# The wait for the last store of a one-core decode kernel, moved from SyncE's instruction stream to GpSimd's

## The chip, the cores and the metric

The kernel runs on one core of one Trainium2 chip. A core has five engines, each with an instruction stream of its own: TensorE (PE), VectorE (DVE), ScalarE (ACT), GpSimd (POOL) and SyncE (SP). They are ordered against each other and against the DMA engines by semaphores alone. The metric is the device time of one execution in microseconds. Beside it stands the span, which is the time from the first to the last instruction of the program in a profile; the device time is longer than the span by what lies before the first and behind the last instruction.

## The reference

The reference is one token of a decode step, a block of cached attention and a small gated mixer behind it. Cut to what matters here:

```python
h  = x + _A_ref(_layernorm(x), k_cache, v_cache, wq, wo)      # 32 query heads, 8 cached heads, 16384 positions of 128
h2 = h + _B_ref(_layernorm(h), w1, w2, w3, w4)                # layernorm, gelu, two products of 512 x 1792
return h2                                                     # shape (1, 1, 512), bfloat16
```

The inputs hold 79 MB that must be read from memory, nearly all of it the two caches. The result is 512 numbers, 1 KB.

## The kernel before

The program is collected as a list of operations for each engine and then emitted (`Program.op` and `Program.emit`). An operation names the tiles it reads (`r`) and writes (`w`); from these the class works out which semaphores it has to wait for. On SyncE, ScalarE and GpSimd the operations stand in the order in which they were collected: `_run` emits, for each operation, the waits that are not yet known to be met, and then the operation. So an operation of an engine comes behind every earlier operation of that engine, and an engine that waits does nothing else.

The work itself is four passes over pairs of cached heads (`PAIRS` is 4). For each pair SyncE loads a 4 MB stretch of keys and one of values; VectorE transposes the keys, TensorE makes the scores, VectorE and ScalarE the softmax, TensorE the product with the values, and GpSimd and ScalarE fold the partial results of each pair but the last. Behind the four pairs come the output projection and the two products of the mixer, with their weights loaded into the space that the keys have left.

All large loads go through SyncE's queue. A SyncE load waits until its target tile is free and is then issued; SyncE carries no arithmetic. GpSimd has little to do: constants and masks at the start, two additions and one product for each of the first three pairs, four instructions that do nothing but wait for the values' landing and raise a semaphore for TensorE (line 499, a `nop`), one such for `od` (line 730), and a power of the variance for each layernorm (line 563). The second of these powers is its last instruction.

The end of the program is this. TensorE's last products (line 844) leave the result in one PSUM bank. ScalarE copies one half of it to the tile `fin` (line 849), VectorE the other (line 851), at the same time. SyncE waits for both and issues the store of `fin` to `out` (line 852). The last operation is a `nop` that reads `out` (line 854): it has no work, and it holds the engine on which it stands until the store's semaphore has its full count. The operation is given the semaphore wait itself, so that it appears as one instruction of the sequencer in the profile.

The functions that the change touches follow.

Of the kernel before, what the change touches and what calls it, by code (L numbers as in the profile page):

```python
# [390 lines left out]
def bass_sequential_preLN__gqa_block_cached__mixer_s_mlp__decode_kernel(  # L391
# [13 lines left out]
    with ExitStack() as ctx:  # L405
        sb = lambda name, shape, dt: ctx.enter_context(nc.sbuf_tensor(name, shape, dt))
        ps = lambda name, shape, dt: ctx.enter_context(nc.psum_tensor(name, shape, dt))
        P = Program(nc, ctx)
# [106 lines left out]
        def piece(cuts, m):  # L515
            return [lo <= m < hi for lo, hi in cuts].index(True)
# [52 lines left out]
        for n, (lo, hi) in enumerate(((0, 2048), (2048, NCH * HQ * DH))):  # L569
# [13 lines left out]
            r=["ident", "x4"], w=["quarter"])  # L583
# [9 lines left out]
             r=["ident_f"], w=["swapped"])  # L593

        dve(lambda e: e.tensor_reduce(row32[:, :], ident_f[:, :].rearrange("p (c r) -> p r c", c=4), AX.X, ALU.add),
            r=["ident_f"], w=["row32"])
        dve(lambda e: e.tensor_reduce(maskdd[:, :], ident_f[:, :].rearrange("p (n d) -> p d n", d=4), AX.X, ALU.add),
            r=["ident_f"], w=["maskdd"])
# [6 lines left out]
        for z, m, key, mk in ((zo, rowgh, "zo", "rowgh"), (zd, maskgh, "zd", "maskgh")):  # L605
# [5 lines left out]
            r=["hT", (("st", 0), 0), (("st", 0), 6)] + [("v", 0), ("v", 1)], w=["xn"])  # L611
# [3 lines left out]
        for i, key in enumerate(keys):  # L615
            P.part("query", i)
            for k in range(NCH):
                pe(lambda e, k=k: e.matmul(row[:, bass.ds(P.b, 512)], copies(xn[:, k:k + 1], 128),  # L618
                                           wq_k[:, k, bass.ds(P.c, REP * DH)], start=(k == 0), stop=(k == NCH - 1)),
                   r=["xn"], also=[("v", 0), ("v", 1)], w=["n" if key == "mn" else key], bank=[key])  # L620
        P.part()
        for g in range(2):
            half = banks[64 * g:64 * g + 64, PAIRS * g:PAIRS * g + PAIRS, :].rearrange("p j c -> p (j c)")
            for b in range(2):
# [3 lines left out]
                    r=["n" if x == "mn" else x for x in keys[PAIRS * g:PAIRS * g + PAIRS]], w=["qcol"],  # L628
# [147 lines left out]
        for n, (lo, hi) in enumerate(W4):  # L776
# [4 lines left out]
            r=[("o_m", j) for j in range(PAIRS)], w=["o_f"])  # L781
# [3 lines left out]
        for r_ in range(32):  # L785
# [3 lines left out]
               r=["o_b", ("r", 0, piece(WO, r_))], w=[("O", 0)], bank=[("O", 0)])  # L789
        h_ps, hkey = banks[:, 6, :], "spare0"  # L790
        dve(lambda e: e.tensor_copy(osum[:, :], O_ps[0][:, :]), r=[("O", 0)], w=["osum"] + [("osum", c) for c in range(4)], bank=[("O", 0)])
        for q in range(4):
            pe(lambda e, q=q: e.matmul(h_ps[32 * q:32 * q + 32, 0:128], copies(row32[:, 0:1], 32),
                                       osum[:, q * 128:(q + 1) * 128], start=True, stop=True),
               r=["osum", "row32"], w=[hkey], bank=[hkey])
# [6 lines left out]
            r=["hT", (S, 0)], w=["hc"])  # L802


        for k in range(NCH):
            for q in range(4):
                pe(lambda e, k=k, q=q: e.matmul(s_ps[32 * q:32 * q + 32, 0, 0:FQ], hc[:, k, :],  # L807
                                                w3_sb[:, k, q * FQ:(q + 1) * FQ], start=(k == 0), stop=(k == NCH - 1)),
                   r=["hc", ("r", 1, piece(W3, k))], w=[("s", 0)], bank=[("s", 0)])
# [3 lines left out]
            r=["hr", "xs", (S, 6)], w=["xsum"])  # L813
        unread_f(384)
        for n in range(2):
# [11 lines left out]
           r=["swapped", "xsum"], w=["n"], bank=["mn"])  # L827
        for m in range(NEAR):
# [3 lines left out]
               r=[("hcol", 2 * m // NHC), ("r", 1, len(W3) + piece(W4, m))], w=[("O", 1)], bank=[("O", 1)])  # L832
        dve(lambda e: e.tensor_copy(osum[:, :], O_ps[1][:, :]), r=[("O", 1)], w=["osum"], bank=[("O", 1)])  # L833
        act(lambda e: e.activation(hg[:, 0:256], hcol[:, 0:8, :].rearrange("p m u -> p (m u)"), ACTF.Identity),
            r=[("hcol", 1)], w=["late", ("hg", 0), ("hg", 1)])
# [6 lines left out]
        for m in range(NEAR, NHC):  # L842
            for o in range(4):
# [4 lines left out]
                   r=["late", ("r", 1, len(W3) + piece(W4, m))], w=["n"], bank=["mn"])  # L848
        act(lambda e: e.activation(fin[:, 0:128], n_ps[0:64, 0:128], ACTF.Identity),
            r=["n"], w=[("fin", 0)], bank=["mn"])  # L850
        dve(lambda e: e.tensor_copy(fin[:, 128:256], n_ps[64:128, 0:128]), r=["n"], w=[("fin", 1)])  # L851
        P.op("SP", lambda e: e.dma_start(out[0, 0:1, :].rearrange("o (q j) -> (o q) j", q=2), fin[31:33, :]),
             r=[("fin", 1), ("fin", 0)], w=["out"], dma="out")
        P.op("SP", lambda e: e.nop(), r=["out"])
        P.emit()

    return nc
# [28 lines left out]
```

## Time and profile before

| What | Value |
|---|---|
| device time, median of 3 runs | 189.55 us |
| the three runs | 189.49, 189.55, 190.38 us |
| device time of the profiled execution | 189.68 us |
| span of the profiled execution | 188.4 us |
| mean granted TensorE clock | 0.900 |
| read from memory | 79.17 MB, 420 GB/s over the span |

The profile is of one execution. Its views give times in microseconds from the start of the span. A "q" behind an engine's name means its sequencer: an instruction that waits, branches or issues a DMA, during which the engine itself stays idle. SyncE has only such instructions. A wait is recorded when it ends: the instruction's start is the time at which its semaphores were met, and its duration is what it took from there. A landing is the time at which a DMA's semaphore had its full count.

### The profile page before, as it was taken

The page shows a single profiled execution, that of the slowest core. Times are in us where ns is not written, and L with a number is a line of the kernel's source. Part 1 is how long each engine was busy: PE and PEld are TensorE (multiplying, and loading weights), DVE is VectorE, ACT ScalarE, POOL GpSimd, SP SyncE. Part 2 cuts the span into 40 slices and gives each one's busy share as a digit, 9 for nine tenths or more (in the row PEclk, how much of TensorE's full clock was granted, in tenths as well). Part 3 has the DMA queues.
Part 4 walks back from the last instruction along what each step waited for, and adds up shares of the span by engine and source line. Part 5 has one row for each costly group of instructions (what it writes and reads, how often), then busy time and mean ns, then how long its engine had stood idle before and what let it go on. Part 6 is the DMA issues. An engine that isn't in the chain of part 4 may idle for free.

```text
span 188.4 us, 2420 instructions
## 1 busy us (share of the span) xinstructions
PE 127.7 (68%) x776; PEld 52.7 (28%) x780; DVE 111.5 (59%) x138; ACT 14.2 (8%) x32; POOL 10.6 (6%) x20
## 2 busy tenths in 40 slices
PE   1019700699965604999775019997986999797974
PEld 1003300243322201344332003432432433353332
DVE  4900751999645009998460069994659895443254
ACT  3000000000020200000112000000220000320012
POOL 1900000000000110000002000000003000000010
PEclk9999995599997975699999756999997899999999
DMA  6999999999999999988999999997999999979994
GB/s 239 457 418 445 445 445 445 445 445 445 445 445 445 445 445 445 417 348 348 445 445 445 445 445 445 445 445 334 445 445 445 557 431 445 431 314 396 419 410 163
DMA packets 2461, 79.19 MB, mean 420 GB/s; under 512 B 282, under 2 KB 284, under 8 KB 924
## 3 DMA queue, kind: packets, MB, share of 16 engines
q1 hardware_dynamic: 2452, 79.17, 97.8%
q8 instruction: 1, 0.02, 0.0%
q10 hardware_dynamic: 8, 0.00, 0.0%
HBM read 79.17 MB, written 0.00 MB: 420 GB/s over the span
## 4 chain that ended last, share of the span: by engine, by line
DMA 66%; DVE 31%; PE 1%; issue 1%; SPq 0%; ACT 0%; DVEq 0%
DMA kb<-in_A_k_cache_dram 53%; DVE kt L641 30%; DMA kb<-in_B_w_dram 13%; PE banks L807 1%; SPq L483 0%; DVE osum L833 0%; PE banks L830 0%; PE banks L844 0%; DVE hcol L821 0%; ACT hg L817 0%; PE banks L838 0%; DVE fin L851 0%; DVEq L159 0%; SPq L159 0%
## 5 line engine op out<-in xcount | busy, mean ns | idle before, releaser
L641 DVE STREAM_TRANSPOSE kt<-kb 128x1024 int32<-128x1024 int32 (+1 forms) x49 | 71.8, 1534 | 31.8 <-DMA kb<-in_A_k_cache_dram 31.8
L660 PE MATMUL banks<-kt,qn 128*128 x256 | 67.8, 414 | 0.0
L660 PEld LDWEIGHTS banks<-kt,qn 128*128 x256 | 26.2, 102 | 40.1 <-issue 21.6
L522 PE MATMUL banks<-xn 128*128 128x512 bf16 x90 | 22.0, 381 | 0.6 <-issue 0.6
L654 PE MATMUL banks<-qn 128*128 128x512 bf16 x8 | 3.7, 465 | 27.0 <-DVE kt L641 26.8
L697 PE MATMUL banks<-vb,pt 128*32 128x512 bf16 x256 | 16.1, 408 | 0.0
L618 PE MATMUL banks<-vb,xn 128*128 x32 | 9.1, 454 | 9.4 <-DVE xn L609 9.4
L682 ACT ACTIVATE p_sb<-banks,bias 128x1024 bf16<-128x1024 f32 x4 | 4.5, 1114 | 126.2 <-DVE nmh L678 126.2
L686 DVE STREAM_TRANSPOSE pt<-p_sb 64x1024 bf16<-64x1024 bf16 x8 | 9.9, 1239 | 5.4 <-ACT p_sb L682 5.3
L522 PEld LDWEIGHTS banks<-xn 128*128 128x128 bf16 x94 | 8.8, 99 | 12.2 <-issue 4.1
L670 DVE TENSOR_REDUCE mx<-banks 128x1 f32<-128x1024 f32 x4 | 4.9, 1225 | 8.9 <-PE banks L660 8.9
L697 PEld LDWEIGHTS banks<-vb,pt 128*32 128x32 bf16 x256 | 7.8, 103 | 6.4 <-issue 1.8
L716 POOL TENSOR_TENSOR osum<-osum 128x256 f32<-128x256 f32 x3 | 2.2, 724 | 126.4 <-ACT osum L713 126.4
L625 DVE STREAM_TRANSPOSE kt<-banks 64x1024 f32<-64x1024 f32 x4 | 4.8, 1228 | 7.2 <-PE banks L618 7.2
L654 PEld LDWEIGHTS banks<-qn 128*128 128x128 bf16 x8 | 0.8, 99 | 29.0 <-issue 28.6
L618 PEld LDWEIGHTS banks<-vb,xn 128*128 128x128 bf16 x32 | 3.6, 112 | 14.5 <-issue 12.1
L732 PE MATMUL banks<-od,zo 128*32 128x128 f32 x8 | 1.6, 285 | 7.3 <-POOL od L718 6.1
L674 PE MATMUL banks<-mxd,mean 128*128 128x128 f32 x8 | 2.0, 326 | 5.3 <-DVE mxd L671 5.3
L713 ACT ACTIVATE osum<-banks,rowc 128x128 f32<-128x128 f32 x12 | 3.4, 368 | 20.6 <-PE banks L697 20.6
L705 PE MATMUL banks<-acc,zd 128*32 128x1 f32 x8 | 0.9, 186 | 4.1 <-DVE pt L686 4.0
L606 DVE COPY zo<-rowgh 128x32 f32<-128x32 f32 x1 | 3.6, 3633 | 0.0
L563 POOL TENSOR_TENSOR st<-st,expo 128x1 f32<-128x1 f32 (+1 forms) x2 | 1.3, 634 | 41.2 <-DVE st L561 41.2
(87 smaller groups left out, 50.9 us busy)
## 6 DMA issues: line engine op xcount, KB each, us to landing
kb<-in_A_k_cache_dram SPq DMA_DIRECT2D x2, 4096.0 KB, 20.5
vb<-in_A_wq_dram SPq DMA_DIRECT2D x1, 3584.0 KB, 11.5
kb<-in_A_wo_dram SPq DMA_DIRECT2D x1, 3584.0 KB, 28.5
kb<-in_B_w_dram SPq DMA_DIRECT2D x1, 1792.0 KB, 24.2
kb<-in_B_w_dram SPq DMA_DIRECT2D x1, 896.0 KB, 26.0
kb<-in_B_w_dram SPq DMA_DIRECT2D x1, 640.0 KB, 27.1
vb<-in_A_wq_dram SPq DMA_DIRECT2D x1, 512.0 KB, 3.4
kb<-in_A_wo_dram SPq DMA_DIRECT2D x1, 512.0 KB, 29.4
```

The lines of the kernel that those rows point to most:

```text
L522: P.unread = lambda e: e.matmul(banks[:, 7, :], copies(xn[:, 0:1], 128), copies(xn[:, 0:1], 512), start=True, stop=True)
L606: dve(lambda e, z=z, m=m: e.tensor_copy(z[:, :].rearrange("p (n d) -> p n d", d=4), m[:, :, :].rearrange("p g h -> p (g h)").unsqueeze(2). ...
L618: pe(lambda e, k=k: e.matmul(row[:, bass.ds(P.b, 512)], copies(xn[:, k:k + 1], 128), wq_k[:, k, bass.ds(P.c, REP * DH)], start=(k == 0), s ...
L625: dve(lambda e, g=g, b=b, half=half: e.transpose(qcol[64 * g:64 * g + 64, 2 * b:2 * b + 2, :, :].rearrange("p e m u -> p (e m u)"), half.r ...
L641: P.op("DVE", lambda e, t=t, n=n, at=at: e.transpose(kt[:, t * KP:(t + n) * KP].bitcast(I32), kb_all[:, at:at + n * KP].bitcast(I32)), r=[ ...
L654: pe(lambda e: e.matmul(row[:, bass.ds(P.y, 512)], copies(none, 128), copies(none, 512), start=True, stop=False, skip_group_check=True), r ...
L660: pe(lambda e, n=n: e.matmul(row[:, bass.ds(P.y, 512)], qn[:, n, bass.ds(P.q, 128)], key_piece(P.k, n), start=False, stop=(n == 3), skip_g ...
L670: dve(lambda e: e.tensor_reduce(mx[:, :], s_all, AX.X, ALU.max), r=[("s", 0), ("s", 1)], w=["mx"], **both)
L682: act(lambda e: e.activation(p_sb[:, :], s_all, ACTF.Exp, bias=bias[:, 0:1], scale=float(SCALE), accum_out=acc[:, :]), r=[("s", 0), ("s", ...
L686: dve(lambda e, g=g: e.transpose(pt[64 * g:64 * g + 64, :, :, g, :], p_sb[64 * g:64 * g + 64, :]), r=["p"], w=["pt"])
L697: pe(lambda e, l=l, ct=ct, ch=ch: e.matmul(O_ps[0][32 * ct:32 * ct + 32, :], pt[:, l, ch, :, :].rearrange("p g u -> p (g u)"), tiles[:, l ...
L713: act(lambda e, c=c: e.activation(osum[:, c * 128:(c + 1) * 128], O[:, c * 128:(c + 1) * 128], ACTF.Identity, scale=rowc[:, c:c + 1]), r=[ ...
```

## The change

The last operation, the `nop` that reads `out`, is collected for GpSimd instead of SyncE. Nothing else differs: the store is still issued by SyncE, through SyncE's queue, and its semaphore is the same.

```diff
         P.op("SP", lambda e: e.dma_start(out[0, 0:1, :].rearrange("o (q j) -> (o q) j", q=2), fin[31:33, :]),
              r=[("fin", 1), ("fin", 0)], w=["out"], dma="out")
-        P.op("SP", lambda e: e.nop(), r=["out"])
+        P.op("POOL", lambda e: e.nop(), r=["out"])
         P.emit()
```

SyncE's stream then ends with the store's issue at line 852. GpSimd's stream ends with the wait, behind the power at line 563.

## Prediction

> **What bounds the kernel now.** I read the page's head and its chain of work first, to see whether the end of the program belongs to what sets the time at all, then the timeline of the last microseconds, then the waits of SyncE, then the single lines that the change touches.
>
> ```profile
> span 188.4 us, 2420 instructions
> DMA 66%; DVE 31%; PE 1%; issue 1%; SPq 0%; ACT 0%; DVEq 0%
> DMA kb<-in_A_k_cache_dram 53%; DVE kt L641 30%; DMA kb<-in_B_w_dram 13%; PE banks L807 1%; SPq L483 0%; DVE osum L833 0%; PE banks L830 0%; PE banks L844 0%; DVE hcol L821 0%; ACT hg L817 0%; PE banks L838 0%; DVE fin L851 0%; DVEq L159 0%;
> q1 hardware_dynamic: 2452, 79.17, 97.8%
> ```
>
> The reader is to see that the kernel is bound by its loads: the queue that SyncE feeds keeps the 16 DMA engines at 97.8% of the span, and the chain is loads and key transposes almost throughout. The change touches no load. It stands entirely behind the last product, so its worth has to be read from the last stretch alone.
>
> ```profile
> 182.21 0.97 PE banks L807 x15
> 183.20 0.50 ACT hg L817
> 184.40 0.63 PE banks L830 x7
> 185.80 0.42 PE banks L838 x8
> 186.22 0.28 PE banks L844 x20
> 186.52 0.33 PE banks L844 x8
> 186.87 0.29 DVE fin L851
> ```
>
> These are pieces of the chain in order of time: start, duration, what. Behind the last load the chain is a strict relay, and it ends with the copy to `fin` at 186.87 + 0.29 = 187.16 us. Only the store comes after that:
>
> ```profile
> 187.21 0.33 SPq L852 DMA_DIRECT2D out_dram<-fin  x1
> SPq L854 <- DMA out_dram<-fin: 0.8, 1, 0.8
> L854 SPq EVENT_SEMAPHORE  x1: 17/17/17, 188.4 to 188.4; - x1
> ```
>
> The first row is of the timeline (start, duration), the second of SyncE's waits (total, times, longest), the third of the view of one source line (shortest, median, longest in ns, then first and last start). SyncE issues the store from 187.21 to 187.54 us. It then sits 0.8 us until the store has landed, at about 188.34, and its last instruction takes 17 ns and ends the span at 188.4. Between the issue and the landing no engine works:
>
> ```profile
> 187.55:188.35 0.80, 0.00 (x0) 0.00 (x0) 0.00 (x0) 0.00 (x0) 0.00 (x0) 0.92 0.01 1
> ```
>
> This is the view by windows: five engines, zero instructions each, then the clock, the DMA share and GB/s. So the last 0.8 us are the store's own flight. Whoever waits for it, it can't land sooner, because it is issued by the same engine from the same place behind the same two copies.
>
> The profiled execution took 189.68 us of device time with a span of 188.4, so 1.3 us lie outside of the span: before the first instruction and behind the last. The profile says nothing on how these 1.3 us are divided or which engine makes them. That is where this change can act, and it is the only place.
>
> **The change part by part.** It removes one sequencer instruction from SyncE, 17 ns at the very end (the row of line 854). Nothing stands behind it on SyncE, so nothing is released earlier inside the program. The wait of 0.8 us doesn't vanish; it is done by GpSimd.
>
> It adds one such instruction to GpSimd. Where GpSimd stands at that time:
>
> ```profile
> 181.97 0.71 POOL L563 TENSOR_TENSOR st<-st,expo 128x2 f32<-128x2 f32 x1 [38.10 <-DVE st L561]
> ```
>
> This is its last instruction and ends at 182.68 us. GpSimd is thus free 182.68 to 188.34, that is 5.7 us, before the store has landed. It can't come late to the wait, and it holds nobody up by standing in it, since no operation of GpSimd follows and no other engine waits for one.
>
> Its cost inside the span is the time from the landing to the end of the waiting instruction, on GpSimd instead of SyncE. GpSimd does the same thing four times already, for the values:
>
> ```profile
> L499 POOLq EVENT_SEMAPHORE  x4: 17/17/17, 51.6 to 168.0; - x4
> L483 SPq DMA_DIRECT2D vb<-in_A_v_cache_dram x1: 328/328/328, 140.1 to 140.1; - x1
> DMA to landing us min/median/max: 27.9/27.9/27.9
> L730 POOLq EVENT_SEMAPHORE  x1: 43/43/43, 173.6 to 173.6; - x1
> ```
>
> The instruction takes 17 ns on GpSimd as on SyncE. The last load of values is issued at 140.1 and lands 27.9 us later, at 168.0, and the fourth wait of line 499 is met at 168.0: with rounding of both rows the reaction is under 0.15 us, and it includes a semaphore update that the new wait doesn't have. The dearest wait of that kind on GpSimd (line 730, on two semaphores, with an update) took 43 ns. So in place of 17 ns the span ends with 17 to 43 ns, and up to 0.15 us if the reaction is as slow as the rounding allows. I take 0.02 us, nearest to line 499, which waits for a DMA's semaphore just like the new one. The other end, below nothing, is excluded but for some nanoseconds, since the landing itself is not moved and SyncE's reaction is only from 188.34 to 188.4.
>
> What lies outside of the span is not shown, so I bound it from both sides. **On the side of a gain:** SyncE now ends its stream at 187.54 instead of 188.37. If SyncE has something of its own to do after its last instruction, it can do that in the 0.8 us of the flight. What it can save is at most 0.8 us from such an overlap, or, if SyncE's closing is longer than that and GpSimd's is nothing, still no more than the 0.83 us by which SyncE ends earlier. It also can't be more than the part of the 1.3 us that lies at the end. So the gain is between nothing and 0.83 us, which puts the lower end of the time at 189.68 - 0.83 = 188.85. **On the side of a loss:** whatever GpSimd does after its last instruction is now hidden by the 5.7 us that it has left, and is exposed after the change. The cover for it is gone completely, since GpSimd becomes the last engine. The nearest rows for the price are those of the program's start, where every engine passes through the same kind of bookkeeping:
>
> ```profile
> L871 POOLq INC_SWDGE_SEM  x1: 27/27/27, 0.1 to 0.1; - x1
> L871 POOLq DRAIN  x1: 187/187/187, 0.3 to 0.3; - x1
> L871 POOLq EVENT_SEMAPHORE  x2: 17/17/17, 0.5 to 0.6; - x2
> L871 SPq DRAIN  x1: 7/7/7, 0.0 to 0.0; - x1
> L871 SPq EVENT_SEMAPHORE  x1: 17/17/17, 0.7 to 0.7; - x1
> L589 POOL MEMSET qb<- 128x2496 bf16 x1 | 2.2, 2178 | 0.0
> ```
>
> SyncE's share of the start is a drain of 7 ns and one wait of 17 ns. GpSimd has a drain of 187 ns, an increment of 27 ns and two waits of 17 ns, 248 ns together. If a closing on GpSimd is as much dearer than one on SyncE as the opening, it costs 248 - 24 = 0.22 us more. Part of that drain is the four memsets that it lets finish, and at the end GpSimd has been idle for 5.7 us, so nothing is in flight: the lower bound is no difference. The far bound is a piece of software work on GpSimd as long as its longest instruction, the 2.2 us of line 589. I take 0.05 us, nearer to nothing than to the 0.22 us, because the waits are equal on both engines and the drain has nothing to drain.
>
> The sum against the profiled execution is 188.37 + 0.02 + 1.31 + 0.05, or 189.75 us. That execution is 0.13 us above the median of the runs, so the forecast for a median is 189.6. The changes of 0.07 us are far below what a measurement of this kernel can tell from no change, about 0.5% or 0.95 us.
>
> The start rows bear out that GpSimd takes part in a barrier of all engines: SyncE's wait of line 871 is met at 0.7, just after GpSimd's at 0.6. The Trainium skill, page "Runtime: NRT & Kernel Launch", section "The ~15µs preamble/postamble breakdown", says that behind the kernel the runtime runs another barrier, which waits for all engines, and that its relay costs 44 ns for each of 8 steps. By that rule an engine that comes last but stands early in the relay would pay up to 8 x 44 = 0.35 us more than one that stands at its end, and the sum would be 190.1 as an estimate; it would also leave SyncE little to gain, as its own clean-up comes only after all engines have met. No row of this trace lies behind the last instruction, so the trace can't confirm it.
>
> **The rivals.** *GpSimd closes slowly.* After its last instruction GpSimd has a closing piece that SyncE lacks, and it now starts at 188.4 instead of 182.7. It decides from the point at which that piece is over 0.95 us longer than SyncE's. For it speaks that it would have been invisible so far, being covered by 5.7 us, and that GpSimd's bookkeeping at the start is ten times SyncE's (248 against 24 ns). Against it speaks that those 248 ns are still far from 0.95 us, and that in the five waits it has in this trace GpSimd reacts as fast as SyncE. Its price is between 0.95 us and the 2.2 us of the longest row, 1.5 in the middle: 189.55 + 1.5 = 191.1 us.
>
> *SyncE closes slowly.* SyncE feeds the one queue that carries 79.17 MB, so it may have more to put in order than the others, and it now starts 0.83 us earlier. The full overlap gives 189.55 - 0.83 = 188.7 us, which is 0.44% and just under the bound; together with the scatter of the runs (189.49 to 190.38) it can come out as faster. For it speaks that 1.3 us outside of the span have to be spent by someone, and SyncE is the one that ends last now. Against it speaks that the closing may need all engines, and then nothing can be done early.
>
> *The change doesn't do what it says.* The end of the program may be held by the store itself, or by something that no engine's last instruction decides, so that the place of the wait is of no account: 189.55, which can't be told from the forecast and is counted with it.
>
> **How the numbers follow.** The forecast, no difference that can be told, gets 0.55 (0.05 of it for the change that does nothing). A slow closing of GpSimd gets 0.30: it rests on a price that no row shows, yet its cover of 5.7 us is the one large quantity that the change removes. An early closing of SyncE gets 0.15 as a faster result, since its bound of 0.83 us leaves it little room beyond 0.5%. The predicted time is 189.6 us. The likeliest case alone has 189.2 to 190.1: SyncE's overlap by half on one side, the 0.22 us of the opening with the 0.15 us of the slow reaction on the other. The range that takes in the other cases goes from 188.6, the full overlap with 0.1 us of scatter, to 191.6, some two thirds of the way from 0.95 to 2.2 us of a slow closing (189.55 + 2.05). Left out are the dearest closings, some 0.10 of the slow case's 0.30, and gains beyond the overlap, 0.03.
>
> **What would show it.** In the profile of the changed kernel line 854 must stand on GpSimd's sequencer with a start of about 188.4 and 17 ns, and SyncE's last row must be line 852, ending at 187.5. The landing must again come about 0.8 us after the issue's end, and the span must stay within 0.05 us of 188.4 once the loads' own scatter is taken off. The test of the rivals is the difference between device time and span: 1.3 us if the forecast holds, 2.3 and more if GpSimd closes slowly, 0.5 if SyncE closes early. The prediction would be wrong if that difference moves by over 0.95 us, or if the span itself is longer because the wait on GpSimd is met late, well behind a landing that comes on time.

## The result, and the profile after

The changed kernel takes 190.19 us in the median of 14 runs, the kernel before 189.66 us in 14 runs. The ratio is 1.0026, with a 95% interval from 1.0015 to 1.0038. So the change makes the kernel slower by about 0.5 us: clear of chance over so many runs, and little over half of the 0.95 us that the prediction had taken as what can be told from no change.

The profiled execution of the changed kernel took 190.17 us, and its span is *shorter* than that of before. The page's first line:

```profile
span 188.2 us, 2420 instructions
```

The timeline of the changed kernel's end (start, duration, what) and the view of the line with the wait (shortest, median, longest in ns, then first and last start):

```profile
186.69 0.27 ACT L849 ACTIVATE fin<-banks 64x128 bf16<-64x128 f32 x1 [1.66 <-PE banks L844]
186.69 0.29 DVE L851 CAST fin<-banks 64x128 bf16<-64x128 f32 x1 [1.12 <-PE banks L844]
187.03 0.33 SPq L852 DMA_DIRECT2D out_dram<-fin  x1
```

```profile
L854 POOLq EVENT_SEMAPHORE  x1: 17/17/17, 188.2 to 188.2; - x1
```

The reader is to see that everything inside the program went as before. The store is issued 0.05 us after the copies end. The issue ends at 187.03 + 0.33 = 187.36, and the wait is met at 188.2, some 0.8 us later, as on SyncE; it takes 17 ns, as on SyncE. What has changed lies behind it. Device time less span was 189.68 - 188.4 = 1.3 us and is now 190.17 - 188.2 = 2.0 us.

This difference is the quantity that the rest goes by. It is known for each execution, with the span rounded to 0.1 us, and it scatters much less than the device time, since the scatter of the loads (spans from 188.0 to 189.2 us in the 14 runs of the changed kernel) drops out of it. It also holds what lies before the first instruction, which no view shows apart. No run below changes anything there, so a difference between two runs is read as one at the end. Over these 14 runs it is 1.90 us in the mean, between 1.81 and 2.00. Below, "the rest" is short for device time less span, with its mean and 95% interval.

### The profile page after: what moved, and what is told of

The parts are those of the page before. It is cut to its first block, busy times and chain, and to the rows that moved or that the text cites. A ratio compares the mean times of both kernels' runs of the same rounds, so it can differ in the third digit from the quotient of the medians.

```text
span 188.2 us, 2420 instructions
## 1 busy us (share of the span) xinstructions
PE 128.0 (68%) x776; PEld 52.6 (28%) x780; DVE 111.5 (59%) x138; ACT 14.2 (8%) x32; POOL 10.6 (6%) x20
## 4 chain that ended last, share of the span: by engine, by line
DMA 52%; DVE 27%; PE 18%; issue 1%; SPq 0%; ACT 0%; DVEq 0%; POOLq 0%
DMA kb<-in_A_k_cache_dram 52%; DVE kt L641 24%; PE banks L660 8%; PE banks L522 4%; PE banks L697 2%; PE banks L787 1%; DVE mx L670 1%; DVE od L727 1%; PE banks L807 1%; PE banks L530 1%; SPq L483 0%; DVE osum L791 0%; DVE osum L833 0%; PE banks L830 0%; PE banks L844 0%
## 5 line engine op out<-in xcount | busy, mean ns | idle before, releaser
L660 PE MATMUL banks<-kt,qn 128*128 x256 | 67.0, 404 | 0.1
L660 PEld LDWEIGHTS banks<-kt,qn 128*128 x256 | 25.7, 100 | 39.8 <-issue 22.9
```

Source lines behind the costliest of these rows:

```text
L660: pe(lambda e, n=n: e.matmul(row[:, bass.ds(P.y, 512)], qn[:, n, bass.ds(P.q, 128)], key_piece(P.k, n), start=False, stop=(n == 3), skip_g ...
```

## The experiments

Every run below changes only what stands behind line 852 of the kernel before. Where GpSimd or another engine is named as waiting, it stands at the place of line 854.

**Which engine waits.** First the kernel before, unchanged, for the scatter of the rest; then the wait on each of the three engines that had not been tried.

```diff
-        P.op("SP", lambda e: e.nop(), r=["out"])
+        P.op("ACT", lambda e: e.nop(), r=["out"])     # then "DVE", then "PE"
```

> The kernel before, unchanged, to get the difference between device time and span over many executions. In the profiled execution of before it was 1.3 us (189.68 - 188.4); in the changed kernel's fourteen it was 1.8 to 2.0 us. Every theory expects 1.2 to 1.4 us here and a ratio of 1.000. If it were 1.8 and more in some executions, the 0.6 us would be scatter and not the change.

> The last wait on ScalarE. Theory 1 (GpSimd has a closing piece of its own that is 0.6 us longer than the others', hidden as long as GpSimd ends early): difference between device time and span 1.2 to 1.4 us, as with SyncE. Theory 2 (behind the program the engines pass a signal along in a fixed order, and an engine that comes last costs more the earlier it stands in that order): each engine has its own value, and the values of the five lie evenly spaced, one step apart; with GpSimd at 1.9 and SyncE at 1.3 at least one of ScalarE, VectorE and TensorE lies at 0.2 us or more from both. Theory 3 (SyncE alone is cheap, since it also issued the store): 1.9 us on every other engine, so 1.9 here.

> The last wait on VectorE. Theory 1 (closing piece of GpSimd alone): difference between device time and span 1.2 to 1.4 us. Theory 2 (fixed order, evenly spaced steps): a value of its own, one step from a neighbour; if VectorE stands between GpSimd and SyncE, 1.6 us. Theory 3 (SyncE alone is cheap): 1.9 us.

> The last wait on TensorE. Theory 1 (closing piece of GpSimd alone): difference between device time and span 1.2 to 1.4 us. Theory 2 (fixed order, evenly spaced steps): a value of its own; if TensorE stands first and SyncE last with GpSimd in the middle, 2.5 us. Theory 3 (SyncE alone is cheap): 1.9 us.

| The engine that waits | runs | the rest, us | ratio to before, 95% interval |
|---|---|---|---|
| SyncE | 12 | 1.33 ± 0.04 | 0.9997 [0.9982, 1.0012] |
| VectorE | 12 | 1.44 ± 0.03 | 1.0008 [0.9988, 1.0027] |
| ScalarE | 12 | 1.50 ± 0.03 | 0.9999 [0.9983, 1.0015] |
| TensorE | 12 | 1.60 ± 0.04 | 1.0023 [1.0007, 1.0039] |
| GpSimd (the changed kernel) | 14 | 1.90 ± 0.04 | 1.0026 [1.0015, 1.0038] |

The 104 executions of the kernel before that were run beside all these experiments have 1.35 us in the mean and lie between 1.26 and 1.47; not one comes near the 1.81 at which GpSimd's begin. In the four sets of runs in which they were taken their means are 1.34 to 1.36. So the 0.57 us between 1.90 and 1.33, or 0.55 against the 1.35 of all 104, are the change's and not scatter. The ratios of device time are a coarser view: those of VectorE and ScalarE can't be told from 1, because the spans scatter by more than the 0.1 to 0.2 us that are in question, and the 1.0023 of TensorE stands for 0.44 us, of which the rest accounts for some 0.25: its spans were longer besides (188.8 us in the median, those of before 188.4), by no more than spans scatter.

What follows: theory 3, that SyncE alone is cheap, falls, since three engines lie between 1.44 and 1.60 and not at 1.9. Theory 1 in its plain form, with 1.2 to 1.4 us on all others, falls too: each engine has its own price. Theory 2 gets a ladder, but not an even one over all five: SyncE, VectorE, ScalarE and TensorE are 0.11, 0.06 and 0.10 us apart, and GpSimd is 0.30 us above the next one. The pattern is a small ladder, with an extra for GpSimd on top. The Trainium skill, page "Trainium Architecture — The Big Picture", section "Naming decoder ring", numbers the engines TensorE 0, ScalarE 1, GpSimd 2, VectorE 3, SyncE 4. The four ordinary engines stand in the measured ladder in the order of this numbering, the highest number lowest, and by it GpSimd would belong between 1.44 and 1.50. The Trainium skill, page "Runtime: NRT & Kernel Launch", section "The ~15µs preamble/postamble breakdown", puts a step of the relay at 44 ns, and it does so for the barrier ahead of the kernel; the ladder measures 0.27 us over four places, 0.07 us for each. Read that way, GpSimd's 0.57 us would be, as an estimate, some 0.14 for its place and 0.43 of its own. That reading isn't shown: four engines fall into such an order, up or down, by chance once in 12 times, and a ladder would also come out if each engine simply took its own time to close.

The profiles show that the wait itself is short on each engine:

```profile
L854 ACTq EVENT_SEMAPHORE  x1: 17/17/17, 188.2 to 188.2; - x1
```

```profile
L854 DVEq EVENT_SEMAPHORE  x1: 21/21/21, 189.1 to 189.1; - x1
```

```profile
L854 PEldq EVENT_SEMAPHORE  x1: 51/51/51, 188.8 to 188.8; - x1
```

Its 17 to 51 ns lie inside the span and are no part of the rest.

**Is it GpSimd's late end, or SyncE's absence, and from when does it count?** Four runs: GpSimd and SyncE both wait; GpSimd gets a last wait that is met about 1.15 us earlier; one that is met just before SyncE's; and the changed kernel with a drain behind the wait.

```diff
+        P.op("POOL", lambda e: e.nop(), r=["out"])                     # wait_on_both
         P.op("SP", lambda e: e.nop(), r=["out"])
```

```diff
+        P.op("POOL", lambda e: e.nop(), r=[("fin", 0), ("fin", 1)])    # pool_early
         P.op("SP", lambda e: e.nop(), r=["out"])
```

```diff
+        for n in range(4):                                             # pool_just_before
+            act(lambda e: e.activation(scr[0:1, 2:3], mean4[0:1, 0:1], ACTF.Identity),
+                r=[("fin", 0), "late2"], w=["late2"])
+        P.op("POOL", lambda e: e.nop(), r=["late2"])
         P.op("SP", lambda e: e.nop(), r=["out"])
```

```diff
-        P.op("SP", lambda e: e.nop(), r=["out"])
+        P.op("POOL", lambda e: e.nop(), r=["out"])                     # pool_drain
+        P.op("POOL", lambda e: e.drain())
```

> GpSimd and SyncE both wait for the store. So far the difference between device time and span was, by the engine that waits: SyncE 1.33, VectorE 1.44, ScalarE 1.50, TensorE 1.60, GpSimd 1.90 us. Theory 1 (GpSimd has something of its own to do after its last instruction, and it is on the path when GpSimd ends last): 1.9 us, as with GpSimd alone, ratio 1.003. Theory 3 (a wait on SyncE is what makes the end cheap): 1.33 us, ratio 1.000.

> SyncE waits for the store as before; GpSimd also gets a last instruction of the same kind, which waits for the two copies to the result's tile and so ends near 187.2, some 1.15 us ahead of the span's end. Theory 1 (the closing of GpSimd starts at its own last instruction and is longer than SyncE's by about 0.6 us): it is hidden again, 1.33 us between device time and span. Rival (a trailing wait on GpSimd makes its closing slow, whenever it is met): 1.9 us.

> SyncE waits for the store as before; GpSimd's last wait is for a chain of four small copies on ScalarE behind the result's copy, so that GpSimd ends some 0.2 us (call it g, it is read from the trace) ahead of SyncE. Theory 1 (own closing, starting at its own last instruction): the difference between device time and span is 1.90 - g, about 1.7 us. Theory 2 alone (nothing starts until the last engine is in, and only that engine's place in the order counts): SyncE is last, so 1.33 us.

> The wait on GpSimd as in the changed kernel, and behind it a drain on GpSimd, which shows in the trace what GpSimd takes to answer that it has nothing in flight. If the 0.4 us that GpSimd costs over its neighbours in the order is such a drain in its closing, the drain here lasts 0.15 to 0.45 us; a second one in the closing then either costs the same again (difference 1.9 us, device time up by the drain's length) or is cheap because GpSimd is awake (difference 1.5 us, device time 190.2 as in the changed kernel). If draining isn't it, the drain lasts under 0.05 us and the difference stays at 1.9 us.

| Run | runs | the rest, us | ratio to before, 95% interval |
|---|---|---|---|
| both wait | 11 | 1.89 ± 0.05 | 1.0034 [1.0022, 1.0046] |
| GpSimd 1.15 us early | 12 | 1.32 ± 0.03 | 0.9996 [0.9985, 1.0007] |
| GpSimd just before | 10 | 2.00 ± 0.05 | 1.0033 [1.0021, 1.0044] |
| wait and drain on GpSimd | 7 | 1.90 ± 0.07 | 1.0035 [1.0020, 1.0050] |

The two waits of the run in which both wait are met at the same time, to 0.01 us:

```profile
L854 POOLq EVENT_SEMAPHORE  x1: 17/17/17, 188.7 to 188.7; - x1
L855 SPq EVENT_SEMAPHORE  x1: 17/17/17, 188.7 to 188.7; - x1
```

With both waiting the rest is GpSimd's, so it is GpSimd's late end that costs, and SyncE's wait saves nothing. With GpSimd early the rest is SyncE's again. The line that GpSimd's wait stands on in that run:

```profile
L854 POOLq EVENT_SEMAPHORE  x1: 43/43/43, 187.2 to 187.2; - x1
```

It is met at 187.2, while the span of that execution ends at 188.4: a trailing wait on GpSimd that is met 1.15 us early costs nothing.

The run with the drain shows what GpSimd answers when it is asked to finish:

```profile
L855 POOLq DRAIN  x1: 41/41/41, 188.3 to 188.3; - x1
```

That is 41 ns, where the drain in the program's start took 187 with memsets in flight. The wait has been merged into the drain, so these 41 ns take the place of 17. The rest stays at 1.90. GpSimd's extra is therefore not such a drain, and it isn't shortened when one has been done just before.

The run with GpSimd just before SyncE is a miss. Its two waits:

```profile
L857 POOLq EVENT_SEMAPHORE  x1: 17/17/17, 188.2 to 188.2; - x1
L858 SPq EVENT_SEMAPHORE  x1: 17/17/17, 188.4 to 188.4; - x1
```

Its own expectation was 1.90 - g with g the 0.25 us by which GpSimd ended ahead of SyncE (188.190 against 188.439 in the trace's nanoseconds), so 1.65 us by theory 1 and 1.33 by theory 2 alone, and it measured 2.00. Either GpSimd's closing doesn't simply start at GpSimd's last instruction, or the four copies on ScalarE that this run needed cost something themselves. The next three runs separate the two.

**GpSimd ahead of SyncE without touching ScalarE, and ScalarE's copies without GpSimd.** Both edits are against the kernel before.

```diff
+        P.op("POOL", lambda e: e.nop(), r=["out"])
         P.op("SP", lambda e: e.nop(), r=["out"])
+        for n in range(6):                             # sp_later_a; 15 in sp_later_b
+            P.op("SP", lambda e: e.drain())
```

```diff
+        for n in range(4):                             # act_chain_only; 2 in act_chain_two
+            act(lambda e: e.activation(scr[0:1, 2:3], mean4[0:1, 0:1], ACTF.Identity),
+                r=[("fin", 0), "late2"], w=["late2"])
         P.op("SP", lambda e: e.nop(), r=["out"])
```

> GpSimd and SyncE both wait for the store, and SyncE then has six drains in a row with nothing to drain, so that it ends some 0.2 to 0.3 us (g, read from the trace) after GpSimd; no other engine is touched. With GpSimd 0.25 us ahead of SyncE, but ScalarE also late, the difference between device time and span came out at 2.0 us, where a closing that simply starts at GpSimd's last instruction gave 1.65. Theory 1 (own closing of GpSimd, starting at its own last instruction): 1.90 - g here, so about 1.65 us, device time as with GpSimd alone (190.2); the 2.0 us were then the late ScalarE's doing. Theory 4 (GpSimd's end costs its full extra, and no less, until it ends something like a microsecond ahead of the last engine, since its part of the closing only goes on when the others have come): 1.9 to 2.0 us here and device time up by g.

> The same with fifteen drains on SyncE, so that it ends some 0.6 us after GpSimd. Theory 1: GpSimd's extra of 0.57 us is all but hidden, 1.33 to 1.40 us between device time and span. Theory 4: still 1.7 to 2.0 us, and device time up by about 0.6 us over GpSimd alone.

> The four small copies on ScalarE behind the result's copy, as in the run with GpSimd just ahead of SyncE, but GpSimd has no last wait and ends at 182.7 as before; SyncE waits for the store. Theory 1 with the measured 1.50 us for ScalarE as the last engine: ScalarE ends 0.3 us ahead of SyncE, so 1.33 us. If the late ScalarE was what raised that run to 2.0 us: 1.5 us and more here. Theory 4: 1.33 us, since GpSimd is early.

The ends of GpSimd and of SyncE in the first of these, and then in the second:

```profile
L854 POOLq EVENT_SEMAPHORE  x1: 17/17/17, 188.3 to 188.3; - x1
...
L857 SPq DRAIN  x6: 7/7/7, 188.3 to 188.5; - x6
```

```profile
L854 POOLq EVENT_SEMAPHORE  x1: 17/17/17, 188.3 to 188.3; - x1
...
L857 SPq DRAIN  x15: 7/7/7, 188.3 to 189.1; - x15
```

| Run | g, us | the rest, us | 1.90 - g, or 1.33 |
|---|---|---|---|
| both wait (above) | 0 | 1.89 ± 0.05 | 1.90 |
| SyncE later by six drains | 0.24 | 1.65 ± 0.03 | 1.66 |
| SyncE later by fifteen drains | 0.70 | 1.35 ± 0.06 | 1.33 |

In nanoseconds of the trace GpSimd ends at 188.294 and SyncE at 188.535 in the first profile (g 0.24), at 188.367 and 189.072 in the second (g 0.70). The rest falls by as much as GpSimd ends ahead, and stops at SyncE's own 1.33. This is theory 1, with the prices of the first table: the execution ends at the later of two times, 1.33 us behind SyncE's last instruction and 1.90 us behind GpSimd's, where both figures count in what lies before the first instruction. Theory 4, which asked for 1.9 to 2.0 and for 1.7 to 2.0, falls. So does theory 2 alone, which has only the last engine count and asked for 1.33 as soon as SyncE is last: 0.24 us ahead GpSimd still costs. And the drains cost the rest nothing, since fifteen of them leave it at SyncE's own. SyncE's drains lengthen the span, so these two kernels are slower as a whole (1.0028 [1.0011, 1.0045] and 1.0032 [1.0013, 1.0051]); what they show is the rest.

The copies on ScalarE alone, with GpSimd early; the last row is from the view of SyncE's wait:

```profile
186.75 0.27 ACT L849 ACTIVATE fin<-banks 64x128 bf16<-64x128 f32 x1 [1.68 <-PE banks L844]
...
187.06 0.90 ACT L855 ACTIVATE scr<-mean 1x1 f32<-1x1 f32 x4
187.09 0.33 SPq L852 DMA_DIRECT2D out_dram<-fin  x1
...
L857 SPq EVENT_SEMAPHORE  x1: 17/17/17, 188.2 to 188.2; - x1
```

The rest was 1.99 ± 0.05 us over 12 runs (ratio 1.0035 [1.0019, 1.0050]), the same 2.00 as with GpSimd just before. So the miss was ScalarE's doing and says nothing on GpSimd. These are four copies of 0.2 us each, and the last ends at 187.06 + 0.90 = 187.96, 0.3 us ahead of SyncE. Why they cost anything was tried with two of them.

> Two small copies on ScalarE behind the result's copy instead of four, GpSimd early, SyncE waits for the store. With four, ScalarE's last instruction ended 0.3 us ahead of SyncE and the difference between device time and span was 1.99 us, so the execution ended 2.29 us after ScalarE's last instruction. If ScalarE has a closing that starts at its last instruction's end, the slope is one: two copies end 0.47 us earlier, so 1.99 - 0.47 = 1.52 us. If the additional instructions as such cost it (a longer stream), it stays near 2.0 us or falls by half of the rise, to 1.66 us. If only a late ScalarE beyond some threshold counts, 1.33 us.

```profile
187.76 0.44 ACT L855 ACTIVATE scr<-mean 1x1 f32<-1x1 f32 x2
187.81 0.33 SPq L852 DMA_DIRECT2D out_dram<-fin  x1
```

Measured: 1.62 ± 0.04 us over 12 runs, ratio 1.0018 [1.0007, 1.0029]. A closing that starts at ScalarE's last instruction gave 1.52, outside of the interval; a cost for each additional instruction gave 1.66, at its edge; a cost that counts only close to the end gave 1.33 and falls. The last of the two copies ends at 188.20, 0.76 us ahead of the span's end (188.96 in nanoseconds), so the execution ends 2.38 us after ScalarE's last copy, where with four it was 2.29. The cost for each instruction fits better, but two points don't settle it, and why ScalarE's late copies cost anything stays open.

## Why the prediction was right, and where its sum was not

**What bounds the kernel and what the change leaves alone: right.** Loads and the chain are as before, the store's flight is 0.8 us on either engine, the waiting instruction takes 17 ns, and GpSimd is in time for it. The span did not grow.

**That the 1.3 us outside of the span are the only place where the change can act: right.** The rest went from 1.33 to 1.90 us, and that is the whole of the result: 0.57 us against the 0.53 us between the medians. By the prediction's own test, 1.3 us for the forecast and 2.3 and more for a slow closing of GpSimd, the measured 1.90 lies between the two and a little nearer to the slow closing.

**The price of GpSimd's closing: the step that was mis-sized.** The prediction took 0.05 us for it, near nothing, "because the waits are equal on both engines and the drain has nothing to drain". Both reasons are true (17 ns each, a drain of 41 ns), and neither bears on it: the closing behind the program costs 0.57 us more with GpSimd as the last engine than with SyncE, and a drain beforehand doesn't change it. The bound taken from the program's start, 0.22 us, was too low as well. So the sum, 0.07 us above before, was short by half a microsecond. The forecast held because 0.57 us stays below the 0.95 us at which it would have been another case, and no row of the prediction put it there: in that the number was lucky. The range held because it was drawn for such a closing. Two slips in its working change nothing: the 188.37 us already hold the 17 ns of the wait that the 0.02 us add, and 2.05 us lie not two thirds of the way from 0.95 to 2.2 but nearly nine tenths. The measured 190.19 us lies just above the likeliest case's own range, which ended at 190.1.

**The rivals.** That GpSimd closes slowly was the right mechanism. Its cover of 5.7 us is what the change takes away, and the runs with GpSimd ahead by 0, 0.24 and 0.70 us show the cover at work; the price put on it, 1.5 us and in no case under 0.95, was far too high. That SyncE closes slowly and would gain by ending 0.83 us earlier is refuted: SyncE is the cheapest of the five engines to end last, and with both waiting nothing is saved. That the place of the wait is of no account is refuted too, by the ladder of the first table.

**The rule of a relay between the engines.** By it an engine that comes last but stands early was to pay up to 0.35 us more. That the 44 ns hold behind the kernel too was the prediction's own step, since the Trainium skill, in the section that it names, gives them for the barrier ahead of it. The ladder is of the right kind and size, with 0.27 us between SyncE and TensorE, though that a relay makes it is not shown, and the rule spoke rightly against a gain on SyncE. It doesn't explain GpSimd, whose 0.57 us are above the 0.35 and 0.30 above the next engine, where the other steps are 0.06 to 0.11.

No experiment gave a version faster than the kernel before. No place of the last wait gave a smaller rest than SyncE.

## What to carry to other kernels

Device time is longer than the span, and by how much depends on which engine waits last: here by 1.3 us with SyncE, 1.4 to 1.6 with VectorE, ScalarE and TensorE, 1.9 with GpSimd. Leave the last wait on SyncE, and let GpSimd finish its share earlier, by the 0.57 us between the two prices or more; 0.70 and 1.15 us were enough here. Where a change touches only the end, look at device time less span over many runs instead of the device time, whose scatter from the loads hides it.

## What the runs showed that was not expected

Each engine has its own price as the last one, down to steps of 0.06 to 0.11 us, and GpSimd's is 0.30 us above the next. What GpSimd does in that time stays open: no view of a profile reaches behind the last instruction, and only a drain like the one measured (41 ns) could be ruled out.

A few tiny copies on ScalarE beside the store's flight, for which no other engine waits, raised the rest from 1.33 us to 1.62 with two and 1.99 with four. So ScalarE's work in the last microsecond was not free here, although it ended 0.3 to 0.8 us before the last wait was met. Small work on the other engines at that place was not tried.
